# Four raw weight buffers in place of two during the attention stage of a fused attention and MoE kernel

## The chip, the cores and the metric

The kernel runs on one core of one Trainium2 chip. The metric is device time in microseconds (us) of one execution. The core has TensorE (PE in the profile, matrix products), VectorE (DVE) and ScalarE (ACT) for work on tiles, GpSimd (POOL), and SyncE (SP), whose queue issues nearly all the DMA transfers here.

## What is computed

Attention over 4 batches of 8 heads (576 positions, head size 64, causal, with a bias from cumulative sums), then two MoE-like layers on the 2304 x 512 result. The weights arrive as 64-bit floats and everything is computed to single-precision accuracy. Cut to what matters:

```python
def _attn_ref(q, k, v, s):
    scores = np.where(causal, -1e9, scale * q @ k.T + np.minimum(bias, 0.0))
    attn = exp(scores - max(scores)); attn /= sum(attn) + 1e-9
    return attn @ v
...
def _moe_ref(x, w1, w2, w3, w_out):
    return (x @ w1) * (x @ w2) @ w3 @ w_out
...
def _moe2_ref(x, w_in, w_out, g_ln):
    h = x @ w_in
    solu = h * softmax(h)
    return (layer_norm(solu) * g_ln) @ w_out
...
x = _attn_ref(...).transpose(0, 2, 1, 3).reshape(2304, 512)
return _moe2_ref(x=_moe_ref(x=x, ...), ...)
```

## The kernel before

**Stages.** The attention runs in 36 steps, one head a step: scores `sc` (L170, or L178 and L179 for later heads) on TensorE, softmax (L192 on VectorE, `L196` exp on ScalarE), normalisation (L225, L226, L233 on VectorE, L231 on ScalarE), transposes `tr` (L265 to L274) copied out to `PT` (L97 on VectorE, L95 on ScalarE), and the product `av` (L298). From step 10 on, pieces of the first MoE layer fill TensorE between these: `ab_unit` multiplies the attention's result by w1 (`a`) and w2 (`b`) at L326. ScalarE copies `a` out to `a_sb` (L338), and VectorE multiplies `b` by it into `g_sb` (L346), which frees the product's buffer in PSUM. After the attention come the last of these units with the product of w3 and w_out (L637), then the second layer: L721, L753, the normalisation, and L847.

**Weight blocks.** Weights come in blocks of 128 x 512 numbers of 64 bits, 512 KB each. `stage` (L398 to L409) takes a tile named `stage` from a pool and issues the load from SyncE's queue at L407. `to_f32` (L360 to L378) makes 32-bit floats of it in place, one scaling on ScalarE (L363) and three steps on VectorE (L369, L370, L374); `split_w` then writes a coarse part (`hi`, L95, ScalarE) and a rest (`lo`, L100, VectorE) as the two W tiles that the matmuls read. The last of these, the rest, frees the raw tile. L369 can only start when the block has landed. For the second layer's blocks `to_f32` writes its result to another tile (`cst`) at L374, which frees the raw tile.

**How many and when.** 16 blocks of w1 and w2 come first, then 8 of w_in, then 8 of the second w_out. The table `PUMP` (L551) says how many conversions are written into each step: one in steps 3, 5 and 6, two in steps 10 to 15, one in step 16, one each in steps 22 to 29, two each in 30 to 33. `pump` (L415) loads ahead as long as fewer blocks are under way than the pool has buffers, converts one, and loads again. After the attention, blocks come from another pool with four buffers (L616).

**What sets the order.** The engines' queues are in order. Which instruction stands where in its queue is decided when the kernel is built, by a scheduler of the framework that works with estimated durations, so an instruction whose input is estimated to be ready sooner is put sooner in its queue. `issue_after` adds an order: a conversion is put behind the first softmax tile of its step.

**GpSimd** has one task beside all this: `split_qk` (L160 to L163) writes the rest of the next head's Q and K (`lo`, L100 on POOL, QK from qk) after ScalarE's `hi` (L95).

Both numbers of buffers are at these lines:

```python
    stg = [at, 2]
...
        raw = stg[0].tile([128, CW, 2], U32, tag="stage", bufs=stg[1], name="stage")
...
        while jobs and len(loaded) < stg[1]:
...
    stg[:] = mp, 4
```

Of the kernel before, what the change touches and what calls it, by code (L numbers as in the profile page):

```python
# [26 lines left out]
def tile_attention_moe(  # L27
# [76 lines left out]
    at = attn_ctx.enter_context(tc.tile_pool(name="at", bufs=1, side="left"))  # L104
# [288 lines left out]
    jobs = []  # L393
    loaded = []

    stg = [at, 2]

    def stage(src):  # L398
        raw = stg[0].tile([128, CW, 2], U32, tag="stage", bufs=stg[1], name="stage")
# [619 lines left out]
```

## Time and profile before

| | us |
|---|---|
| median of 3 runs | 738.95 |
| the runs | 737.88 to 739.62 |
| the profiled execution | 737.73 |
| its span, first to last instruction | 736.0 |
| PE busy | 716.7 (97%) |
| DVE busy | 504.9 (69%) |
| ACT busy | 468.0 (64%) |
| POOL busy | 99.5 (14%) |

The granted TensorE clock is 0.997 of full speed over the span. A share of busy time is a mean over stages with different limits; what ends a wait in one stage is read from that stage's rows. In a row of a timeline, the brackets at the end give how long the engine stood idle before the instruction and what ended that idle time. "issue" there means that it waited for nothing that the profile shows.

### The profile page before, as it was taken

The numbers are of one execution on the slowest core, as the hardware profiler recorded it, in microseconds if no ns is written. First come the engines' busy times: TensorE is split into PE (matmuls) and PEld (weight loads), VectorE is DVE, ScalarE is ACT, GpSimd is POOL, SyncE is SP. The second block draws the span as 40 slices with busy tenths as digits, with TensorE's granted clock in tenths as the row PEclk, the third lists the DMA queues.
The fourth block names the chain that finished last, engine by engine and source line by source line (L and its number), as shares of the span: only waits on it lengthen the run. The fifth ranks groups of instructions, "written<-read, shape, count | busy, mean of one in ns | idle before, by whom it ended". The sixth has DMA issues, their size and how long they took to land.

```text
span 736.0 us, 13040 instructions
## 1 busy us (share of the span) xinstructions
PE 716.7 (97%) x4682; PEld 625.0 (85%) x4682; DVE 504.9 (69%) x1267; ACT 468.0 (64%) x985; POOL 99.5 (14%) x102
## 2 busy tenths in 40 slices
PE   9889998999999999999998999999999999999997
PEld 6567978888888899899997889988888988888886
DVE  7987978897678888632887876576747365563651
ACT  4987777898766777732544745577646465564652
POOL 5033313142221331000000000001000000000000
PEclk9999999999999999999999999999999999999999
DMA  4644554655476665614566943253234142304221
GB/s 109 186 126 99 174 161 142 194 144 130 127 221 186 182 188 149 208 61 147 170 215 202 355 149 101 58 110 75 79 82 101 44 123 75 89 12 75 44 57 44
DMA packets 79829, 95.52 MB, mean 130 GB/s; under 512 B 41418, under 2 KB 52682, under 8 KB 79764
## 3 DMA queue, kind: packets, MB, share of 16 engines
q1 hardware_dynamic: 79764, 94.69, 45.0%
q8 instruction: 37, 0.61, 0.3%
q14 instruction: 28, 0.23, 0.1%
HBM read 59.04 MB, written 20.14 MB: 108 GB/s over the span
## 4 chain that ended last, share of the span: by engine, by line
PE 73%; DVE 11%; DMA 8%; ACT 5%; issue 2%; POOL 1%; SPq 0%; ACTq 0%; DVEq 0%; POOLq 0%
PE x L721 14%; PE o L847 13%; PE b L326 10%; PE a L326 10%; PE hX L753 5%; DMA stage<-in_w_dram 5%; PE av L298 4%; PE hZ L753 3%; PE tr L265 3%; ACT P L196 2%; PE sc L170 2%; PE sc L178 2%; DVE P L192 2%; DVE stage L374 2%; PE hW L753 2%
## 5 line engine op out<-in xcount | busy, mean ns | idle before, releaser
L196 ACT ACTIVATE P<-P,STAT 128x576 f32<-128x576 f32 (+4 forms) x160 | 88.3, 554 | 31.5 <-DVE STAT L192 30.9
L100 POOL TENSOR_TENSOR QK<-qk,QK 64x1152 fp32r<-64x1152 f32 x24 | 67.1, 2798 | 167.2 <-ACT QK L95 158.9
L721 PE MATMUL x<-gl,MH 128*128 128x256 f32 x288 | 80.4, 280 | 0.0
L721 PE MATMUL x<-gh,ML 128*128 128x256 f32 x288 | 80.2, 279 | 0.0
L721 PE MATMUL x<-gh,MH 128*128 128x256 f32 x288 | 79.9, 280 | 0.0
L192 DVE CUSTOM_DVE_ANT_0 P<-sc,wmask 128x576 f32<-128x576 f32 (+4 forms) x160 | 70.6, 478 | 4.5 <-PE sc L170 3.2
L326 PE MATMUL a<-xT0h,W 128*128 128x288 f32 x256 | 58.1, 300 | 1.9 <-ACT a_sb L338 1.9
L326 PE MATMUL b<-xT0h,W 128*128 128x288 f32 x256 | 57.6, 299 | 1.5 <-DVE STAT L192 0.8
L847 PE MATMUL o<-OH,lh 128*128 128x512 f32 x144 | 57.1, 397 | 0.2 <-DVE ll L100 0.2
L326 PE MATMUL a<-xT1h,W 128*128 128x288 f32 x256 | 57.2, 298 | 0.0
L847 PE MATMUL o<-OH,ll 128*128 128x512 f32 x144 | 57.0, 396 | 0.0
L847 PE MATMUL o<-OL,lh 128*128 128x512 f32 x144 | 57.0, 396 | 0.0
L326 PE MATMUL b<-xT1h,W 128*128 128x288 f32 x256 | 56.5, 295 | 0.0
L721 PEld LDWEIGHTS x<-gl,MH 128*128 128x128 f32 x288 | 54.2, 188 | 1.3
L817 DVE COPY lt<-turned 128x2048 uint16<-128x2048 uint16 x16 | 21.9, 1368 | 48.4 <-DMA turned<-half 48.4
L721 PEld LDWEIGHTS x<-gh,MH 128*128 128x128 f32 x288 | 54.0, 188 | 1.1
L721 PEld LDWEIGHTS x<-gh,ML 128*128 128x128 f32 x288 | 54.1, 188 | 0.9
L346 DVE TENSOR_TENSOR g_sb<-b,a_sb 128x288 f32<-128x288 f32 x64 | 28.8, 449 | 32.8 <-PE b L326 16.7
L363 ACT ACTIVATE stage<-stage 128x512 f32<-128x512 f32 x56 | 36.9, 674 | 21.2 <-DMA stage<-in_w_dram 18.0
L298 PE MATMUL av<-PT,VT 128*64 128x64 f32 (+4 forms) x384 | 50.1, 395 | 0.0
L231 ACT ACTIVATE P<-P,STAT 128x576 f32<-128x576 f32 x64 | 42.7, 717 | 10.4 <-DVE STAT L226 10.4
L338 ACT ACTIVATE a_sb<-a 128x288 f32<-128x288 f32 x64 | 25.6, 401 | 33.3 <-PE a L326 33.1
(193 smaller groups left out, 1965.5 us busy)
## 6 DMA issues: line engine op xcount, KB each, us to landing
stage<-in_w_dram SPq DMA_DIRECT2D x32, 512.0 KB
g_scr<-g_sb SPq DMA_DIRECT2D x32, 288.0 KB
stage<-in_wo_dram SPq DMA_DIRECT2D x16, 512.0 KB
qk<-in_qk_dram SPq DMA_DIRECT2D x24, 288.0 KB
QK<-QK SPq DMA_DIRECT2D x24, 288.0 KB
gl<-g_scr SPq DMA_DIRECT2D x24, 256.0 KB
wf<-wf_scr SPq DMA_DIRECT2D x22, 256.0 KB
out_dram<-o SPq DMA_DIRECT2D x18, 256.0 KB
```

The lines of the kernel that those rows point to most:

```text
L100: eng.tensor_tensor(out=dst, in0=src, in1=hi_.bitcast(F32), op=ALU.subtract)
L192: mx = nc.vector.tensor_tensor_reduce(out=dst2, in0=ps_in, in1=msk, scale=-SCALE, scalar=BIG, op0=ALU.add, op1=ALU.min, accum_out=st[0:row ...
L196: ex = nc.scalar.activation(out=dst, in_=dst, func=AF.Exp, bias=st[0:rows, ti:ti + 1], scale=-1.0, accum_out=st[0:rows, 5 + ti:6 + ti],)
L231: nc.scalar.activation(out=dst, in_=dst, func=AF.Copy, scale=r)
L298: nc.tensor.matmul(st["ps"][64 * e:64 * e + 64, 448 + c0:448 + c1], vr[:, j, e], PT[(2 * p + e) % 4][:, o + c0:o + c1], **kw,)
L326: nc.tensor.matmul(ps, w_[:, c, fs], x_[:, c, sl], start=(c == 0 and w_ is WH and x_ is XH), stop=(c == KC - 1 and w_ is WL),)
L338: ab_last[0] = nc.scalar.activation(out=a_sb, in_=ps, func=AF.Copy).ins
L346: ab_last[1] = nc.vector.tensor_tensor(out=g[:, sl], in0=ps, in1=st["a"], op=ALU.mult).ins
L363: nc.scalar.activation(out=high.bitcast(F32), in_=high.bitcast(F32), func=AF.Copy, scale=2.0 ** -112)
L721: last = nc.tensor.matmul(ps[:, a], w_[:, k, m * 128:m * 128 + 128], g_[:, k % 2], start=(k == 0 and w_ is MH and g_ is GH), stop=(k == KF ...
L753: last_h[0] = nc.tensor.matmul(ps, x_[:, k], w_[:, k], start=first and k == 0 and x_ is XH and w_ is WH, stop=k == 1 and x_ is XL, skip_gr ...
L847: nc.tensor.matmul(ps, l_[:, k], w_[:, k], start=(k == 0 and l_ is LH and w_ is OH), stop=(k == KF - 1 and l_ is LL),)
```

## The change

One number: the pool of the attention stage gives the raw weight tiles four buffers in place of two. The loads ahead follow the same number (L413), so up to four blocks are under way.

```diff
-    stg = [at, 2]
+    stg = [at, 4]
```

No instruction of the work is added or removed. The first row of block loads in SyncE's queue holds four loads where it held two, ahead of the same rows of the next head, and later loads stand two blocks earlier. The scheduler's order of the conversions moves as well. Three places in VectorE's queue follow. Each W pair is named by its two tiles (W_123 the coarse part, W_124 the rest).

The first is the stretch before the g_sb at 88.97 us of the profile. Before:

```order
L192 ISA STAT_117 64x1
L100 TENSOR_TENSOR W_124<-stage,W_123 128x4x128
L192 ISA P,STAT_117<-sc,wmask 128x320
L192 ISA STAT_117 128x1
L192 ISA P,STAT_117<-sc,wmask 128x192
L192 ISA STAT_117 128x1
L100 TENSOR_TENSOR W_122<-stage,W_121 128x4x128
L346 TENSOR_TENSOR g_sb<-b,a_sb 128x288
```

And now:

```order
L192 ISA STAT_117 64x1
L370 SCALAR_TENSOR_TENSOR stage<-stage 128x512
L192 ISA P,STAT_117<-sc,wmask 128x320
L192 ISA STAT_117 128x1
L192 ISA P,STAT_117<-sc,wmask 128x192
L192 ISA STAT_117 128x1
L370 SCALAR_TENSOR_TENSOR stage<-stage 128x512
L100 TENSOR_TENSOR W_122<-stage,W_121 128x4x128
L374 SCALAR_TENSOR_TENSOR stage<-stage 128x512 x2
L346 TENSOR_TENSOR g_sb<-b,a_sb 128x288
```

Two L370 and two L374 of the next two blocks (numbers 8 and 9) now stand ahead of the g_sb; their two L369 stand ahead of it too, some rows earlier, together with the L100 of W_124. Before, all six stood behind it.

The second is some ten rows later, at 93 to 95 us, a piece of the difference with - for before and + for now:

```order
+L100 TENSOR_TENSOR W_124<-stage,W_123 128x4x128
+L97 COPY PT_111<-tr 64x64
+L100 TENSOR_TENSOR W_126<-stage,W_125 128x4x128
+L97 COPY PT_111<-tr 64x2x64
 L233 TENSOR_SCALAR P<-P,STAT_117 128x320
 L233 TENSOR_SCALAR P<-P,STAT_117 128x192
 L233 TENSOR_SCALAR P<-P,STAT_117 64x64
-L97 COPY PT_111<-tr 64x64
-L97 COPY PT_111<-tr 64x2x64
-L374 SCALAR_TENSOR_TENSOR stage<-stage 128x512
```

The two L100 that end blocks 8 and 9 stand here now, where before a step L374 of block 8 stood; the next L374 stands behind the next g_sb now and stood ahead of it.

The third is at 132 to 136 us, the stretch around two g_sb. Before:

```order
L369 TENSOR_SCALAR stage<-stage 128x512
L346 TENSOR_TENSOR g_sb<-b,a_sb 128x288
L369 TENSOR_SCALAR stage<-stage 128x512
L346 TENSOR_TENSOR g_sb<-b,a_sb 128x288
L97 COPY PT_111<-tr 128x512
```

And now:

```order
L97 COPY PT_111<-tr 128x512
L369 TENSOR_SCALAR stage<-stage 128x512
L100 TENSOR_TENSOR W_128<-stage,W_127 128x4x128
L346 TENSOR_TENSOR g_sb<-b,a_sb 128x288
L100 TENSOR_TENSOR W_126<-stage,W_125 128x4x128
L346 TENSOR_TENSOR g_sb<-b,a_sb 128x288
```

The copy of the transposes moved ahead, and an L100 of a block whose other steps are done stands ahead of each g_sb, where an L369 stood ahead of each.

## Rows read from the trace of the kernel before

**Rows 1.** the page, busy time of each engine, share of the span, instructions

```profile
PE 716.7 (97%) x4682; PEld 625.0 (85%) x4682; DVE 504.9 (69%) x1267; ACT 468.0 (64%) x985; POOL 99.5 (14%) x102
```

**Rows 2.** busy time in two stretches: us, then each engine, clock, DMA share

```profile
60.00:165.00 105.00, 99.71 (x759) 88.78 (x757) 89.45 (x260) 85.62 (x215) 28.36 (x10) 1.00 0.54 156
165.00:300.00 135.00, 135.00 (x1066) 120.60 (x1063) 104.25 (x310) 102.12 (x256) 33.44 (x13) 1.00 0.61 174
```

**Rows 3.** waits from 60 to 165 us: total us, times, longest us

```profile
DVE stage L369 <- DMA stage<-in_w_dram: 10.0, 8, 3.1
...
ACT stage L363 <- DMA stage<-in_w_dram: 4.1, 3, 2.8
```

**Rows 4.** TensorE in order: start us, us, operation [idle before <-releaser]

```profile
89.47 0.40 PE L326 MATMUL b<-xT0h,W 128*128 128x288 f32 x1 [0.65 <-DVE g_sb L346]
...
123.76 0.37 PE L178 MATMUL sc<-QK 128*128 128x288 f32 x1 [1.60 <-issue]
...
125.20 0.40 PE L326 MATMUL a<-xT0h,W 128*128 128x288 f32 x1 [0.67 <-ACT a_sb L338]
...
134.83 0.41 PE L274 MATMUL tr<-ident,P 64*64 64x64 f32 x4 [0.42 <-DVE g_sb L346]
...
310.96 0.40 PE L326 MATMUL a<-xT0h,W 128*128 128x288 f32 x1 [1.20 <-ACT a_sb L338]
```

**Rows 5.** steps on a block: duration in ns, min/median/max

```profile
L369 DVE TENSOR_SCALAR stage<-stage x56: 382/422/2034, 22.3 to 431.3; 128x512 uint32<-128x512 uint32 x56
L363 ACT ACTIVATE stage<-stage x56: 647/668/766, 24.6 to 429.5; 128x512 f32<-128x512 f32 x56
L370 DVE SCALAR_TENSOR_TENSOR stage<-stage x56: 642/684/821, 25.3 to 432.8; 128x512 uint32<-128x512 uint32 x56
L374 DVE SCALAR_TENSOR_TENSOR stage<-stage x40: 673/685/1848, 26.0 to 434.6; 128x512 uint32<-128x512 uint32 x40
...
L100 DVE TENSOR_TENSOR W<-stage,W x16: 643/677/2461, 29.0 to 155.0; 128x512 fp32r<-128x512 f32 x16
```

**Rows 6.** VectorE in order of time, 77 to 89 us

```profile
77.99 0.43 DVE L369 TENSOR_SCALAR stage<-stage 128x512 uint32<-128x512 uint32 x1 [0.83 <-DMA stage<-in_w_dram]
...
84.02 1.96 DVE L100 TENSOR_TENSOR W<-stage,W 128x512 fp32r<-128x512 f32 x1
...
86.59 2.46 DVE L100 TENSOR_TENSOR W<-stage,W 128x512 fp32r<-128x512 f32 x1
88.97 0.44 DVE L346 TENSOR_TENSOR g_sb<-b,a_sb 128x288 f32<-128x288 f32 x1
```

**Rows 7.** GpSimd in order of time

```profile
82.74 5.76 POOL L100 TENSOR_TENSOR QK<-qk,QK 64x1152 fp32r<-64x1152 f32 x2 [13.42 <-ACT QK L95]
...
131.46 2.67 POOL L100 TENSOR_TENSOR QK<-qk,QK 64x1152 fp32r<-64x1152 f32 x1 [4.06 <-ACT QK L95]
```

**Rows 8.** chain of waits from 60 to 165 us: start us, us, what

```profile
89.08 3.98 DMA stage<-in_w_dram
```

**Rows 9.** VectorE in order of time, 93 to 133 us

```profile
93.08 0.43 DVE L369 TENSOR_SCALAR stage<-stage 128x512 uint32<-128x512 uint32 x1 [0.53 <-DMA stage<-in_w_dram]
...
105.47 0.47 DVE L369 TENSOR_SCALAR stage<-stage 128x512 uint32<-128x512 uint32 x1 [1.18 <-DMA stage<-in_w_dram]
109.05 0.43 DVE L369 TENSOR_SCALAR stage<-stage 128x512 uint32<-128x512 uint32 x1 [3.11 <-DMA stage<-in_w_dram]
...
122.91 0.74 DVE L192 CUSTOM_DVE_ANT_0 P<-sc,wmask 128x576 f32<-128x576 f32 x1
...
132.38 2.03 DVE L369 TENSOR_SCALAR stage<-stage 128x512 uint32<-128x512 uint32 x1 [1.64 <-DMA stage<-in_w_dram]
```

**Rows 10.** ScalarE at 310 us

```profile
309.93 0.68 ACT L363 ACTIVATE stage<-stage 128x512 f32<-128x512 f32 x1 [1.33 <-DMA stage<-in_wo_dram]
```

**Rows 11.** SyncE's DMA queue, then TensorE, on the early load

```profile
18.97 0.47 SPq L129 DMA_DIRECT2D qk<-in_qk_dram  x1
...
29.91 1.13 PE L170 MATMUL sc<-qk 128*128 128x288 f32 x4
```

## The prediction

> **What bounds the kernel now.** I read the busy shares first: TensorE is busy 716.7 us of a 736.0 us span [rows 1]. Nothing can gain more than the 19.3 us in which it stands still, and of these only the part that raw weight blocks cause. So I next read the stretches. From 60 to 165 us, where thirteen of the sixteen w1 and w2 blocks are converted, PE is busy 99.71 of 105.00 us: 5.29 us idle. From 165 to 300 us, with further blocks converted beside it, it is busy 135.00 of 135.00 [rows 2]. An added buffer can gain nothing in that second stretch; a delay made before it is carried through it whole, since PE has no pause in which to catch up.
>
> The waits of the first stretch come next: VectorE stands 10.0 us before L369, ScalarE 4.1 us before L363, each for a weight block to land [rows 3]. That is the wait which the change removes, 14.1 us on two engines, but PE is idle only 5.29 us there. The list of PE's pauses says what it waited for: 0.65 us at 89.47 for the eviction g_sb, 1.60 at 123.76 (named "issue"; VectorE's L192 beside it, 122.91 plus 0.74, ends 0.11 us earlier [rows 9]), 0.67 at 125.20 for a_sb, 0.42 at 134.83 for g_sb; later, 1.20 at 310.96 for a_sb [rows 4]. PE never waits for a weight block itself. It waits for an eviction that stands behind a conversion in VectorE's or ScalarE's queue, and these queues are in order. The longest block wait, 3.11 us at 109.05 [rows 9], has no pause of PE beside it. So the time is decided by what stands ahead of an eviction, and the change moves that too.
>
> **The change part by part.** The same loads and conversions are issued; only their order differs. A block is four steps on VectorE and two on ScalarE; their median durations are in [rows 5]. I cost places, not totals. My unit is PE's idle time, before and after, and each difference goes into the end one for one, because of the full stretch behind.
>
> *First loads.* Two more blocks are issued at 18 us, ahead of the rows qk of the next head. Those are issued at 18.97 and the first product that reads them starts at 29.91 [rows 11]: 10.94 us. One block took 3.98 us from issue to use in the chain of waits [rows 8]; alone on the queue two more cost at most 7.96, and that head's own load, if it takes no more than such a block, makes 11.94 of it: between nothing and 1.0 us late. I take nothing: the transfers run on 16 engines at once, and 3.98 includes a latency that is not paid twice.
>
> *Around 89 us (term a).* In the new order blocks 8 and 9 are converted ahead of the g_sb that PE's pause at 89.47 waits for. Ahead of it now stand two L369 (0.42 each), two L370 (0.68) and two L374 (0.69), 3.58 us [rows 5]; the block wait of 0.83 at 77.99 goes [rows 6], net 2.75. This must be weighed against GpSimd. Two VectorE steps L100 there took 1.96 and 2.46 us [rows 6] where such a step's median is 0.68 [rows 5], and they end as GpSimd's two L100 do (82.74 plus 5.76 is 88.50) [rows 7]: VectorE was held for 3.06 us. Behind 88.50 the new order still has the second L370, one L100, two L374 and the g_sb: 0.68 + 0.68 + 1.37 + 0.37 = 3.10, so g_sb ends at 91.6 and not at 89.34 (88.97 plus 0.37, where the next step starts): +2.26. If ScalarE's two L363 that now stand before the next QK step put GpSimd off by their 2 x 0.67 = 1.34 [rows 5], it is +3.6; if the second L370 slips in ahead of GpSimd's second step, +1.6. I take the middle, **+2.6**.
>
> The Trainium skill ("SBUF — State Buffer", section Who interferes with whom) says that a VectorE instruction with two SBUF inputs and a GpSimd instruction that reads SBUF block each other entirely, the later one waiting for the whole of the earlier. The two long L100 agree with it; no row before shows an L370 so held, though it has two SBUF inputs as well. By that rule a is +2.26 or more; if an L370 is not held, the second one runs inside the hold and a is its 0.68 less, +1.6.
>
> *From 90 to 107 us (term b).* Between that g_sb and the next pauses the order gains two L100 (2 x 0.68) and loses two L374 (2 x 0.69), which is even. What is left is a wait: block 11 can be loaded only when block 7's L100 frees its buffer, which still stands just before the g_sb, at about 90.5. A load takes 3.98 [rows 8], so it lands near 94.5, and VectorE reaches its L369 between 93.3 and 93.9: 0.6 to 1.2 us of waiting where there were 0.53 at 93.08 [rows 9]. Middle **+0.4**, ends 0 and +1.5 (a hold by GpSimd that falls on one of the L100: 1.96 less 0.68 is 1.3).
>
> *From 105 to 126 us (term c).* By now loads are two blocks further ahead, and the waits of 1.18 and 3.11 us at 105.47 and 109.05 go [rows 9]. VectorE reaches its L192 of 122.91 earlier, and the 1.60 and 0.67 us of PE go: **-2.27**. This also pays for a part of the lag from a: VectorE, which was late by a, catches up in 4.29 us of former waiting, PE does not. Ends: -2.27, and -1.60 where only the first goes.
>
> *Around 134 us (term d).* VectorE waited 1.64 us there and its L369 then took 2.03 (GpSimd ran from 131.46 for 2.67) [rows 7, 9]; both go, but an L100 is put ahead of the two g_sb, and could be held in its place. PE's 0.42 may go, or grow by up to a whole hold, 2.67. I take **0**, ends -0.4 and +2.7.
>
> *Around 311 us (term e).* ScalarE waits 1.33 us for a block of the second w_out in front of the a_sb that PE waits 1.20 us for [rows 10, 4]. The last of these loads also come two blocks earlier in the order, and the wait goes: **-1.2**, ends -1.2 and 0 (another wait takes its place).
>
> The blocks after the attention had four buffers already; their waits stay. Sum: 2.6 + 0.4 - 2.27 + 0 - 1.2 = -0.47. The profiled execution took 737.73 us, 1.7 of it outside the span; it would take 737.3. The median of the runs lies 1.22 above the profiled one, 738.95, so the forecast for it is **738.5 us**. With all lows the sum is 1.6 + 0 - 2.27 - 0.4 - 1.2 = -2.3, with all highs but d (3.6 + 1.5 - 1.6 + 0 + 0) +3.5: this case's own range is 736.7 to 742.5.
>
> **The rivals.**
> *Every load-made pause goes, no new one comes.* VectorE has 105.00 - 89.45 = 15.55 us free in the stretch [rows 2], more than all moved steps take; if the early conversions only use free time, all 5.29 us and the 1.20 us go: -6.5, 732.5 us; with half of it, 735.7. For it: the waits of 10.0 and 4.1 us. Against it: at 77 to 89 us, where blocks 8 and 9 are put, VectorE has no free time but the 0.83.
>
> *Earlier conversions delay evictions: slower.* A conversion that is ready sooner is put in the queue sooner, among softmax tiles and ahead of g_sb. Place: 81 to 89 us, with GpSimd's 5.76 us; price: a at 3.6, b at 1.5, and d at +2.7, less c and e at their small end, -1.6 and 0: +6.2 at worst, 745.2; with d at 0, +3.5, 742.5. It decides once a and b together exceed 3.5 us, what c and e together give back. For it: 135 us without a pause in which a lag could shrink. Against it: VectorE gets 4.29 us back at 105 to 109.
>
> *The waits were hidden anyway.* PE's pauses then come from the order of evictions alone and reappear elsewhere: 0, 738.95.
>
> That the change does nothing it says (the loads not issued earlier) I leave at nothing: the order shows four loads in the first row where there were two.
>
> **How the numbers follow.** About 0.2%, 1.5 us, is what a measurement of this kernel can tell from no change; same is 737.5 to 740.4. Chances: my forecast 0.45, of which 0.11 ends below 737.5 and 0.10 above 740.4; every pause goes 0.25, all faster; slower 0.23, all slower; waits hidden anyway 0.07, same. Faster 0.36, same 0.31, slower 0.33. The range leaves out the lower part of the first rival (below 734.6) and the upper part of the second (above 742.8), a tenth each: 734.6 to 742.8. Both signs hold most of the chance, so the likeliest case's own range, 736.7 to 742.5, is to be kept beside it.
>
> **What would show it.** The waits before L369 for w1 and w2 blocks from 60 to 165 us fall from 10.0 to at most 2 us: if not, the loads are late for another reason. The g_sb behind blocks 8 and 9 ends 1.6 to 3.6 us later against its PE step, and PE pauses there for more than 2 us: if it pauses under 1 us, term a is wrong, and the first rival holds. An L370 or L374 of 1.8 us or more lies beside GpSimd's L100. The pauses at 123.76, 125.20 and 310.96 are gone: if one stays, c or e is wrong. PE still has none between 165 and 300 us; if it has, the delay is not carried one for one, and the whole sum is wrong.

## The result and the profile after

With four buffers the kernel is slower. The median of 6 runs is 743.73 us (740.96 to 745.29), against 738.82 us (6 runs) for the kernel before; the ratio is 1.0063, 95% interval 1.0041 to 1.0084. The profiled execution took 742.21 us, its span is 740.4 us against 736.0.

Of the page of the changed kernel, the busy time of each engine (answers [rows 1]), and below it two stretches with the same columns as [rows 2]:

```profile
PE 720.1 (97%) x4682; PEld 629.0 (85%) x4682; DVE 508.2 (69%) x1267; ACT 467.6 (63%) x985; POOL 98.8 (13%) x102
...
60.00:165.00 105.00, 96.89 (x708) 86.14 (x705) 88.42 (x246) 81.09 (x199) 25.36 (x9) 0.95 0.52 154
165.00:300.00 135.00, 135.00 (x1064) 122.00 (x1063) 105.59 (x309) 102.19 (x258) 35.71 (x13) 1.00 0.57 162
```

The same 4682 matmuls are busy for 720.1 us in place of 716.7. So in this pair of executions, of the 4.4 us by which the span grew, 3.4 are matmuls that ran slower and only 1.0 is time in which PE stood still (20.3 us in place of 19.3). The column behind the five engines goes with it: the granted clock is 0.95 in the first stretch, where it was 1.00. How far this holds beyond this pair is asked in the first experiment.

The waits for weight blocks are gone as forecast: between 60 and 165 us no wait for a load stands before an L369 or an L363 any more [rows 3]. The waits list of that stretch (total us, times, longest us) now has, among others, these:

```profile
PE b L326 <- DVE g_sb L346: 5.5, 2, 2.8
ACT W L95 <- DVE stage L374: 5.0, 5, 2.4
```

TensorE's pauses, in order of time, as in [rows 4]:

```profile
80.91 0.47 PE L178 MATMUL sc<-QK 128*128 128x448 f32 x1 [0.93 <-DVE g_sb L346]
...
93.38 0.40 PE L326 MATMUL b<-xT0h,W 128*128 128x288 f32 x1 [2.65 <-DVE g_sb L346]
...
107.45 0.40 PE L326 MATMUL b<-xT0h,W 128*128 128x288 f32 x1 [1.71 <-DVE STAT L192]
...
132.35 0.58 PE L326 MATMUL b<-xT0h,W 128*128 128x288 f32 x1 [2.81 <-DVE g_sb L346]
```

The small pauses of before have become one of 0.93 us and three long ones. The first is a matter of place alone: its g_sb stood ahead of an L370 and an L374 before (at 79.10 us, with no pause of PE) and stands behind them now (at 80.41), and GpSimd runs nothing beside them. For the three long ones, VectorE's rows ahead of them show what is late, and GpSimd's rows what ran beside it (start, us, operation):

```profile
85.39 2.70 DVE L370 SCALAR_TENSOR_TENSOR stage<-stage 128x512 uint32<-128x512 uint32 x1
...
88.70 2.45 DVE L370 SCALAR_TENSOR_TENSOR stage<-stage 128x512 uint32<-128x512 uint32 x1
...
92.88 0.44 DVE L346 TENSOR_TENSOR g_sb<-b,a_sb 128x288 f32<-128x288 f32 x1
...
103.48 2.70 DVE L374 SCALAR_TENSOR_TENSOR stage<-stage 128x512 uint32<-128x512 uint32 x1
...
126.39 3.17 DVE L374 SCALAR_TENSOR_TENSOR stage<-stage 128x512 uint32<-128x512 uint32 x1
```

```profile
84.84 5.75 POOL L100 TENSOR_TENSOR QK<-qk,QK 64x1152 fp32r<-64x1152 f32 x2 [15.07 <-ACT QK L95]
102.36 3.27 POOL L100 TENSOR_TENSOR QK<-qk,QK 64x1152 fp32r<-64x1152 f32 x1 [11.76 <-ACT QK L95]
...
126.06 2.95 POOL L100 TENSOR_TENSOR QK<-qk,QK 64x1152 fp32r<-64x1152 f32 x1 [2.92 <-ACT QK L95]
```

Each long step of VectorE, 0.68 us by its median [rows 5], lies beside one GpSimd instruction and ends 0.55 us behind its end. Ahead of the first pause two L370 are held, ahead of the second an L374, ahead of the third another.

The clock ahead of the pauses and behind them, by stretches with the columns of [rows 2]; the column behind POOL's is the granted clock, and 0.50 is its lower level, 1.2 GHz. First the changed kernel, then the kernel before:

```profile
90.70:93.30 2.60, 0.03 (x1) 0.00 (x0) 2.60 (x6) 1.90 (x7) 0.00 (x0) 1.00 0.20 60
...
94.10:97.40 3.30, 3.30 (x16) 3.30 (x15) 2.85 (x13) 2.70 (x6) 0.00 (x0) 0.50 0.63 199
97.50:98.10 0.60, 0.60 (x7) 0.60 (x6) 0.60 (x3) 0.41 (x1) 0.00 (x0) 1.00 0.00 0
...
132.40:138.40 6.00, 6.00 (x25) 5.79 (x26) 6.00 (x13) 4.38 (x8) 1.45 (x1) 0.50 0.48 135
```

```profile
89.40:92.70 3.30, 3.23 (x24) 3.23 (x25) 3.14 (x14) 3.30 (x11) 0.00 (x0) 1.00 0.88 231
...
396.50:400.00 3.50, 3.50 (x10) 2.71 (x9) 3.04 (x6) 2.41 (x4) 0.00 (x0) 0.51 0.37 114
```

In 3.3 us PE does 16 matmuls where it did 24. Behind the pause at 93.38 the same run of work, from the first matmul of that `b` to the first matmul of the next `b`, goes from 93.38 to 98.19 (4.81 us); before it went from 89.47 to 92.76 (3.29 us). The lower clock costs 1.52 us there. The last row shows that the trace of before had the pattern already, behind its longest pause, 2.05 us at 395.72. The changed kernel has that stretch too, near 401 us, and one more at 53 to 56 us, which cost little, since PE waited 1.05 us there before and does no more.

How far the last transposes (L267) of some heads lie behind the kernel before:

| start before, us | start after, us | later by, us |
|---|---|---|
| 62.70 | 63.15 | 0.45 |
| 88.41 | 89.21 | 0.79 |
| 97.03 | 102.46 | 5.44 |
| 121.61 | 126.65 | 5.04 |
| 134.16 | 142.23 | 8.07 |
| 165.38 | 172.27 | 6.89 |
| 208.41 | 214.99 | 6.57 |
| 309.35 | 315.92 | 6.57 |
| 320.32 | 325.51 | 5.19 |
| 494.47 (L847) | 498.95 | 4.48 |

The loss is made twice, at 88 to 97 and at 122 to 134 us. The 0.79 us understates the lag there: four score products (L178 and L179, 89.38 to 90.31) stand behind that L267 now and stood ahead of it before, and the last matmul of `a` ahead of both lies 1.29 us behind (87.85 against 86.56). Of the 8.07 us 1.5 come back by 208 us; nothing of the 6.57 that are left is given back through the rest of the full stretch; 1.38 come back at 311 us, where the pause of 1.20 [rows 4] is gone, and 0.7 more later.

### The profile page after: what moved, and what is told of

It is laid out like the page before. It is cut to its first block, busy times and chain, and to the rows that moved or that the text cites. A ratio compares the mean times of both kernels' runs of the same rounds, so it can differ in the third digit from the quotient of the medians.

```text
span 740.4 us, 13031 instructions
## 1 busy us (share of the span) xinstructions
PE 720.1 (97%) x4682; PEld 629.0 (85%) x4682; DVE 508.2 (69%) x1267; ACT 467.6 (63%) x985; POOL 98.8 (13%) x102
## 4 chain that ended last, share of the span: by engine, by line
PE 89%; DVE 6%; ACT 2%; issue 2%; POOL 1%; DMA 0%; SPq 0%; ACTq 0%; POOLq 0%
PE x L721 14%; PE o L847 13%; PE b L326 13%; PE a L326 13%; PE av L298 6%; PE m L637 6%; PE hX L753 5%; PE tr L265 4%; PE hZ L753 3%; PE sc L178 2%; PE sc L170 2%; PE sc L179 2%; PE hW L753 2%; PE hY L753 2%; DVE stage L374 1%
## 5 line engine op out<-in xcount | busy, mean ns | idle before, releaser
L100 POOL TENSOR_TENSOR QK<-qk,QK 64x1152 fp32r<-64x1152 f32 x24 | 66.4, 2769 | 174.1 <-ACT QK L95 174.0
L192 DVE CUSTOM_DVE_ANT_0 P<-sc,wmask 128x576 f32<-128x576 f32 (+4 forms) x160 | 70.6, 479 | 6.4 <-PE sc L170 3.6
L326 PE MATMUL a<-xT0h,W 128*128 128x288 f32 x256 | 59.7, 306 | 0.0
L847 PE MATMUL o<-OH,lh 128*128 128x512 f32 x144 | 57.0, 396 | 0.2 <-DVE ll L100 0.2
L847 PE MATMUL o<-OH,ll 128*128 128x512 f32 x144 | 57.0, 396 | 0.0
L847 PE MATMUL o<-OL,lh 128*128 128x512 f32 x144 | 57.0, 396 | 0.0
L326 PEld LDWEIGHTS b<-xT0h,W 128*128 128x128 f32 x256 | 43.6, 191 | 8.3 <-ACT PT L95 3.0
```

The costliest lines, as they stand in the source:

```text
L100: eng.tensor_tensor(out=dst, in0=src, in1=hi_.bitcast(F32), op=ALU.subtract)
L192: mx = nc.vector.tensor_tensor_reduce(out=dst2, in0=ps_in, in1=msk, scale=-SCALE, scalar=BIG, op0=ALU.add, op1=ALU.min, accum_out=st[0:row ...
L326: nc.tensor.matmul(ps, w_[:, c, fs], x_[:, c, sl], start=(c == 0 and w_ is WH and x_ is XH), stop=(c == KC - 1 and w_ is WL),)
L847: nc.tensor.matmul(ps, l_[:, k], w_[:, k], start=(k == 0 and l_ is LH and w_ is OH), stop=(k == KF - 1 and l_ is LL),)
```

## Experiments

The theory after the result: the loads are harmless, and the order that they allow puts two-input VectorE steps beside GpSimd's L100 and ahead of evictions; these holds make pauses of PE, and the clock falls behind some long pauses. A step is called held when it takes longer than its median beside a GpSimd instruction. Ratios below are to the kernel before as measured beside each run, with 95% intervals; medians of different runs come from different chips, so the ratios are compared. All kernels whose text says nothing else compute everything.

**Are the loads to blame?** Four buffers, two blocks loaded ahead. VectorE's, TensorE's and GpSimd's orders stay those of the changed kernel; only SyncE's rows differ.

```diff
-        while jobs and len(loaded) < stg[1]:
+        while jobs and len(loaded) < (2 if stg[0] is at else stg[1]):
```

> Four buffers as in the changed kernel, but only two blocks are loaded ahead where the program asks for loads: SyncE's first row of block loads holds two, and the order on VectorE, TensorE and GpSimd is that of the changed kernel. Theory (the order of the conversions makes the kernel slower, not the loads): 743 to 745 us, and the pauses of TensorE near 93, 107 and 132 us stay. Rival (the earlier loads disturb something): 738 to 740 us, with those pauses gone or halved.

Measured: 742.66 us, 1.0047 (1.0028 to 1.0066), and the pauses stay: 2.38 at 93.50, 2.15 at 108.03 and 2.81 at 132.91. The number is a little under what the theory said, the loss is the same within the intervals. The four loads at 18 us are not the cause.

This run also weighs the clock, since the orders of the engines are those of the changed kernel. Its profiled execution has a span of 740.9 us, and its busy times are:

```profile
PE 717.7 (97%) x4682; PEld 626.2 (85%) x4682; DVE 508.5 (69%) x1267; ACT 467.9 (63%) x985; POOL 98.2 (13%) x102
```

The three pauses are there, but behind the one at 132.91 the clock stays up (1.00 from 133 to 140 us). The span is 4.9 us longer than before, and of these only 1.0 is busy time and 3.9 are idle. So nearly the whole loss comes without that stretch of lower clock, and the 3.4 of 4.4 us above belong to one pair of executions, with granted clocks of 0.997 and 0.988 over the span. The mean over all runs differs less: 0.990 for the six of the changed kernel, 0.992 for the ten of this run, 0.993 to 0.994 for the kernel before beside the experiments.

**Is it the hold or the place?** GpSimd's L100 on Q and K becomes a fill that reads nothing, in the changed kernel and in the kernel before.

```diff
-        lo(t[64:128, 1::2], raw, t[64:128, 0::2], G)
+        nc.gpsimd.memset(t[64:128, 1::2].bitcast(F32), 0.0)
```

> The changed kernel with GpSimd's L100, which reads SBUF and computes the rest of Q and K, replaced by a fill of the same tile with zeros, which reads nothing: the rest is left out, so scores are rougher. VectorE's order is that of the changed kernel but for a few rows. Theory (the moved L370 and L374 cost much because GpSimd holds them, and long pauses of TensorE bring its clock down): no L370 or L374 over 1 us, the pauses near 93, 107 and 132 us shrink by 1.5 to 2 us each, the stretches at half clock go, 735 to 739 us. Rival (their place alone, in front of evictions): pauses shrink by less than 0.7 us each and 742 to 744 us.

> The kernel before with the same replacement of GpSimd's L100 by a fill with zeros (the rest of Q and K is left out). VectorE's order is that of the kernel before but for a few rows. Theory: the held L100 (1.96, 2.46 and 1.79 us) go back to 0.7, but PE pauses there are short, so only 0.5 to 2 us are gained: 736.5 to 738.5 us; and the changed kernel without GpSimd's reads is as fast as this one or up to 3 us faster. Rival (place alone): 737 to 739, and the changed kernel without the reads stays 4 us or more above it.

Measured: 735.37 us, 0.9954 (0.9934 to 0.9974), for the changed order; 737.24 us, 0.9967 (0.9936 to 0.9998), for the order of before. In the first of these kernels the L370 and the g_sb that follows are:

```profile
85.05 0.68 DVE L370 SCALAR_TENSOR_TENSOR stage<-stage 128x512 uint32<-128x512 uint32 x1
...
86.34 0.68 DVE L370 SCALAR_TENSOR_TENSOR stage<-stage 128x512 uint32<-128x512 uint32 x1
...
88.76 0.44 DVE L346 TENSOR_TENSOR g_sb<-b,a_sb 128x288 f32<-128x288 f32 x1
```

The g_sb comes 4.12 us earlier than at 92.88, and PE has no pause there. The changed kernel gained 1.1% by the fill, the kernel before 0.3%. So in sum the place alone costs nothing: with the fill the changed order is level with the order of before or slightly ahead. At one spot the place does cost: the pause of 0.93 us at 80.91 stays (0.94 at 80.57). And one part of the forecast failed. Instead of a smaller pause near 107 us with the clock up, the profiled execution, the slowest of its ten, has this one, with the clock at half from 100.5 to about 107 us:

```profile
100.52 0.63 PE L274 MATMUL tr<-ident,P 64*64 64x64 f32 x4 [2.03 <-DVE STAT L192]
```

Ahead of it VectorE waited 2.37 us for a weight block, at 93.90; that this wait made the pause is not shown.

These two kernels leave work out, and the fill is also shorter (1.05 to 1.24 us where the L100 took 2.7 to 3.3), so the next pair does all of the work.

**Short holds with all the work.** GpSimd's instruction is issued as eight pieces. In the changed kernel VectorE's order stays as it was up to 160 us; in the kernel before it differs in some rows from 90 us on. (The new line is broken in two here.)

```diff
-        lo(t[64:128, 1::2], raw, t[64:128, 0::2], G)
+        [lo(t[64:128, 1 + 2 * i, s_], raw[:, i, s_], t[64:128, 2 * i, s_], G)
+         for i in range(2) for s_ in (slice(c, c + S // 4) for c in range(0, S, S // 4))]
```

> The changed kernel, complete, with GpSimd's L100 on Q and K issued as eight pieces of 64x144 in place of one of 64x1152; VectorE's order up to 160 us is that of the changed kernel. Theory (a VectorE step is held until the GpSimd instruction beside it ends): each hold falls from up to 2.7 us to the rest of one piece, no L370 or L374 over 1.2 us, the pauses near 93, 107 and 132 us lose 1.5 us each, 736 to 739 us. Rival (what the kernel without GpSimd's reads gained came from the computation it left out, or from Q and K being ready sooner): 742 us or more, since GpSimd then takes as long as before or longer.

> The kernel before with the same eight pieces on GpSimd. Theory: its holds fall too, but few pauses of PE hang on them: 737 to 738.5 us, 0.3 to 1.5 us faster than before. Together with the changed kernel in eight pieces: the change is then worth between 1 us slower and 2 us faster. Rival (the change costs time by its place alone): the two in eight pieces stay 4 us or more apart.

Measured: 734.48 us, 0.9936 (0.9914 to 0.9957), with four buffers, faster than both kernels; 740.02 us, 1.0012 (0.9987 to 1.0037), with two. The first is better than forecast; the second gained nothing where 0.3 to 1.5 us were forecast; and the change is worth 5.5 us between the two, by their medians, where 2 at most were. For VectorE and GpSimd in the first kernel (start, us, operation):

```profile
85.30 0.68 DVE L370 SCALAR_TENSOR_TENSOR stage<-stage 128x512 uint32<-128x512 uint32 x1
...
86.59 0.76 DVE L370 SCALAR_TENSOR_TENSOR stage<-stage 128x512 uint32<-128x512 uint32 x1
87.27 0.98 DVE L100 TENSOR_TENSOR W<-stage,W 128x512 fp32r<-128x512 f32 x1
88.17 1.87 DVE L374 SCALAR_TENSOR_TENSOR stage<-stage 128x512 uint32<-128x512 uint32 x2
89.97 0.44 DVE L346 TENSOR_TENSOR g_sb<-b,a_sb 128x288 f32<-128x288 f32 x1
```

```profile
84.75 10.30 POOL L100 TENSOR_TENSOR QK<-qk,QK 64x144 fp32r<-64x144 f32 x16 [13.15 <-ACT QK L95]
```

GpSimd now needs 10.30 us for what took 5.75, and the kernel is faster: VectorE's steps run between the pieces or are held for one of them only, and GpSimd has time. That Q and K were ready sooner can't be the reason here, as it could with the fill: GpSimd ends later (95.05 us) than in the changed kernel (90.59). With two buffers VectorE's waits before L369 grow instead, in a listing by line from 60 to 170 us (count, busy us and mean ns, idle before and its releaser), the kernel in pieces below the kernel before:

```profile
L369 DVE TENSOR_SCALAR stage<-stage 128x512 uint32<-128x512 uint32 x13 | 7.3, 568 | 10.1 <-DMA stage<-in_w_dram 10.0
```

```profile
L369 DVE TENSOR_SCALAR stage<-stage 128x512 uint32<-128x512 uint32 x13 | 6.2, 486 | 15.1 <-DMA stage<-in_w_dram 15.1
```

That two buffers in pieces gain nothing because VectorE then waits for loads is argued from these two rows and not shown: no run takes these waits away by itself, VectorE's order differs from 90 us on, and in this execution the clock is also at half from 53.5 to 60.5 and from 128.5 to 132.5 us, where it is up in the kernel before. What is shown is that the two changes don't add: buffers alone lose 0.6%, pieces alone change nothing that can be told, both together gain 0.6%.

**How short must a piece be?** Two pieces, VectorE's order as in the changed kernel.

> The changed kernel with two pieces on GpSimd in place of one; VectorE's order is that of the changed kernel. Theory (a hold is the rest of one GpSimd instruction): holds up to 1.4 us, less than half the gain of the eight pieces kept at most, between 735 and 740 us, and no pause over 2 us. If GpSimd's next piece follows before VectorE gets in, the hold is two pieces and the time that of the changed kernel, 742 to 744 us.

Measured: 742.53 us, 1.0067 (1.0052 to 1.0082; 4 runs), all of the changed kernel's time; the second expectation holds in its number, though not by its mechanism. GpSimd and the held steps:

```profile
86.72 6.91 POOL L100 TENSOR_TENSOR QK<-qk,QK 64x576 fp32r<-64x576 f32 x4 [14.93 <-ACT QK L95]
```

```profile
90.47 1.90 DVE L100 TENSOR_TENSOR W<-stage,W 128x512 fp32r<-128x512 f32 x1
92.30 2.49 DVE L374 SCALAR_TENSOR_TENSOR stage<-stage 128x512 uint32<-128x512 uint32 x2
```

No step is held for two pieces: the two L370 take 1.44 and 1.24 us. But the L100 and the first L374 (1.89 us) are held now too, which ran free behind GpSimd's end in the changed kernel. The work alternates, and with pieces of 1.7 us (6.91 by four) the holds ahead of g_sb, less 0.68 us a step, come to the same sum, 3.75 us against 3.79; PE's pause is 2.35 us.

**Which holds?** Four buffers and eight pieces, but at named heads the whole instruction; VectorE's order is that of the kernel in eight pieces up to 160 us. The heads in the condition change from run to run; the last run has `h in (11, 12, 13, 15)`.

```diff
         for i in range(2) for s_ in (slice(c, c + S // 4) for c in range(0, S, S // 4))]
+        if h not in (15,) else lo(t[64:128, 1::2], raw, t[64:128, 0::2], G)
```

> Four buffers and eight pieces on GpSimd for all heads but one, head 15, whose L100 is one whole instruction again: it is the one that lay beside the held L374 of 3.17 us at 126.39 in the changed kernel. VectorE's order is that of the kernel in eight pieces. Theory (one hold at one place makes the pause of 2.81 us at 132, and the pause brings the half clock behind it): one L374 of about 3 us, a pause of 2 to 3 us near 130, the clock at half for 3 to 7 us behind it, and 2.5 to 5 us more than the kernel in eight pieces, 737 to 739.5 us. Rival (the holds act only together): under 1.5 us more, 734.5 to 736 us.

> The same with heads 11 and 12 whole, whose two L100 hold the two L370 of blocks 8 and 9 at 85 to 91 us in the changed kernel. Theory: the L370 take 2.4 to 2.7 us again, the pause near 93 is 2 to 2.7 us with the half clock behind it, 2 to 4.5 us more than the kernel in eight pieces, 736.5 to 739 us; less if the free time of VectorE at 110 to 120 us takes a part back. Rival (the holds act only together): under 1.5 us more.

> Eight pieces on GpSimd but for head 13, whole. Theory (each held place costs its pause, 1 to 3 us): an L374 of about 2.7 us near 101, a pause of PE near 104 of 1 to 2 us, 1 to 2.5 us more than the 734.5 us of the kernel in eight pieces. Rival (only holds together): under 1 us more.

> Eight pieces but for heads 11, 12, 13 and 15, whole. If the places add up: 1.2 + 2.9 + 1 to 2.5 us above 734.5, 739.6 to 741.1 us. If they build on each other, by a later start of every step behind and by the clock: 742 to 744 us, all of the changed kernel's time. If the rest lies at other heads: 737 to 739 us.

> Whole at all heads but 11, 12, 13 and 15, which are in eight pieces. If these four places carry the loss: 734 to 736 us. If other heads carry it: 738 us or more.

| whole at heads | median, us | ratio (95%) | above 0.9936 |
|---|---|---|---|
| 15 | 735.72 | 0.9970 (0.9952 to 0.9988) | 0.34% |
| 11, 12 | 737.42 | 0.9986 (0.9967 to 1.0005) | 0.50% |
| 13 | 735.56 | 0.9960 (0.9942 to 0.9977) | 0.24% |
| 11, 12, 13, 15 | 740.55 | 1.0029 (1.0007 to 1.0050) | 0.93% |
| all but these four | 736.66 | 0.9969 (0.9953 to 0.9984) | 0.33% |
| all (the changed kernel) | 743.73 | 1.0063 (1.0041 to 1.0084) | 1.27% |

The places add as far as this can tell: 0.34 + 0.50 + 0.24 is 1.08 against 0.93, and 0.93 + 0.33 is 1.26 against 1.27; but each ratio has an interval of about 0.2% to either side, so single places are rough. By these ratios the four places carry about three quarters. The four together, 740.55 us, lie in the range for places that add up. Head 15 alone missed its forecast: 735.72 us lies in the range of the rival, 734.5 to 736. Heads 15 and 13 cost 1.2 and 1.1 us by medians, 2.5 and 1.8 by ratios, the low end of what was expected or below it, and the kernel with these four in pieces at 736.66 lay between the two expectations. Head 15 alone made its pause, but with the clock up behind it (the last row, with the columns of [rows 2]):

```profile
128.47 0.37 PE L326 MATMUL b<-xT0h,W 128*128 128x288 f32 x1 [2.31 <-DVE g_sb L346]
```

```profile
128.50:132.00 3.50, 3.50 (x27) 3.41 (x28) 3.50 (x9) 2.44 (x6) 0.00 (x0) 1.00 0.29 91
```

So the half clock doesn't follow every pause of that length; with heads 11 and 12 whole it does follow a pause of 2.29 us (0.50 from 93 to 96 us). Which pauses it follows stays open.

**Three buffers**, whole and in eight pieces.

```diff
-    stg = [at, 4]
+    stg = [at, 3]
```

> Three buffers. The first L370, L370 and L374 in the crowded stretch stand as in the changed kernel, but only one block, not two, is put ahead of the g_sb that PE's b waits for near 90 us, and later places lie between the two kernels. Theory (the number of two-input steps put beside GpSimd and ahead of g_sb decides): between the two, 739.5 to 742.5 us. Rival (any look-ahead beyond two costs the same): 743 to 745 us.

> Three buffers with eight pieces on GpSimd. Theory: three buffers already were near the kernel before because their holds make no long pause; with short holds they come to 734 to 736.5 us, as four buffers with eight pieces do. Rival (the fourth buffer is needed for the gain): 737 us or more.

Measured: 737.79 us, 0.9986 (0.9969 to 1.0003), and 732.91 us, 0.9945 (0.9927 to 0.9963). The first is a miss: three buffers are not between the two kernels but level with the kernel before. Ahead of the g_sb of 92 us two steps are held there too, an L370 for 2.44 us at 85.39 and an L100 for 2.46 at 88.44, but no more than in the kernel before (two L100, 1.96 and 2.46 us [rows 6]), and PE pauses 0.26 us for that g_sb. The longest pause between 60 and 165 us is 1.63 us, and the clock stays at full speed behind it. Within the intervals three buffers in pieces are as fast as four; the fourth is not needed.

**Other places for the conversions.** In both kernels four buffers, the table of conversions changed.

```diff
-    PUMP = {3: 1, 5: 1, 6: 1, 10: 2, 11: 2, 12: 2, 13: 2, 14: 2, 15: 2, 16: 1}
+    PUMP = {3: 1, 4: 1, 5: 1, 6: 1, 7: 2, 8: 2, 9: 2, 10: 1, 11: 1, 12: 1, 13: 1, 14: 1, 15: 1}
```

> Four buffers, and the table that says how many conversions are written into each step is spread: one in steps 4 to 6 each and step 3, two in steps 7 to 9, one in steps 10 to 15, where it was none in steps 4 and 7 to 9 and two in steps 10 to 15. Theory (too many conversions at once in the crowded stretch from 76 to 140 us): the pauses near 93, 107 and 132 us go, no half clock after 60 us, 733 to 737 us. Rival (earlier loads and conversions as such make it slower): 743 us or more.

```diff
-    PUMP = {3: 1, 5: 1, 6: 1, 10: 2, 11: 2, 12: 2, 13: 2, 14: 2, 15: 2, 16: 1}
+    PUMP = {3: 1, 5: 1, 6: 1, 10: 2, 11: 2, 13: 2, 14: 2, 15: 2, 16: 2, 17: 1}
```

> Four buffers, and the conversions of steps 12 to 16 written one step later (steps 13 to 17). Ahead of the g_sb near 89 us then stand one L374 and two L100 of earlier blocks, about as in the kernel before, while loads stay four ahead. Theory (place and hold decide): the pause at 93 us falls to under 1.2 us, with no half clock behind it; 739 to 742 us, since L370 and L374 still meet GpSimd near 125 us. Rival (four buffers and early loads cost by themselves): 743 to 745 us.

Measured: 741.92 us, 1.0027 (1.0007 to 1.0048), and 742.17 us, 1.0049 (1.0018 to 1.0080). The first is a miss. The pauses near 93 and 107 us are gone and that at 132 falls to 1.19, as forecast, but the loss has moved to where the conversions went: 2.75 us at 58.14 before `tr`, with VectorE's copies behind conversions, and half clock from there to 67 us, where none was forecast after 60. The second, 0.2 us above its range, removes the first long pause (0.45 is left at 93.64) and gets two others: 2.35 at 120.96, released by GpSimd's QK, and 2.82 at 124.94, released by the W of an L95, so by a block that is now converted too late. Why QK came late in the first of them stays open. This run doesn't tell the theory from its rival.

## Why the prediction was wrong

**The bound and the full stretch: right.** The waits for blocks went to nothing, PE still has no pause from 165 to 300 us, and from 208 to 309 us the lag is carried unchanged. Term e was -1.2 and measured -1.38.

**Term a: the mechanism right, one consequence missing.** The g_sb ended 3.91 us later (93.25 against 89.34), 2.6 to 3.1 after the lag of 0.79 to 1.29 that was there already: inside 1.6 to 3.6. The L370 were held, 2.70 and 2.45 us, and the runs in pieces and with the fill take the holds away. The Trainium skill ("SBUF — State Buffer", section Who interferes with whom) has it so for a step with two SBUF inputs beside a GpSimd instruction that reads SBUF, and the trace agrees. PE's pause grew by 2.0 us. What the sum lacked is the clock, 1.5 us behind this pause in the profiled execution, and the new pause of 0.93 us at 80.91.

**Term b** was +0.4; from 97 to 122 us, the stretch of b and the first part of c, the lag changed by -0.4. The wait for block 11 on which it rested did not come.

**Term c is the step that failed.** It took PE's pauses of 1.60 and 0.67 us for gone, -2.27. They went, but a longer one came. The same L374 stands beside the same GpSimd instruction in both kernels. Before, it started 0.22 us ahead of it, took 0.68 us (the first of the two in this row), and GpSimd's instruction took 3.59:

```profile
123.59 1.28 DVE L374 SCALAR_TENSOR_TENSOR stage<-stage 128x512 uint32<-128x512 uint32 x2
```

```profile
123.81 3.59 POOL L100 TENSOR_TENSOR QK<-qk,QK 64x1152 fp32r<-64x1152 f32 x1 [6.03 <-ACT QK L95]
```

Now it starts at 126.39, 0.33 us behind GpSimd's start at 126.06, and is held for 3.17 us ahead of the next g_sb. PE paused for 2.81 us and then, in this execution, ran at half clock until 138.4. Where c had -2.27, the lag grew by 3.0 from 122 to 134 us. I had weighed the moved steps against GpSimd's rows at 83 and 131 us only; the order showed moved L370 and L374 at every head between.

**Term d** was 0; the pause of 0.42 us went, its low end, and the lag fell by 0.7 to 144 us and by 0.8 more to 208.

**The clock had no term at all.** The kernel before shows the lower level once, behind its pause of 2.05 us at 395.72, so it could have been priced. In the profiled pair 3.4 of the 4.4 us are busy time, but the run with two blocks ahead loses 4.9 us with 1.0 of busy time: idle time makes most of that loss, and what the clock costs on average was not measured.

By the lag in the table, the sum of -0.47 became 4.48. Term c alone missed by 5.3 us (3.0 in place of -2.27) and term a by about 2 (4.65 from 88 to 97 us in place of 2.6); the rest went the other way. The second rival, that earlier conversions delay evictions, had the mechanism, and its 742.5 to 745.2 us hold the median; but it put the loss at 81 to 89 us and counted c as a gain of 1.6, so its meeting the number is partly luck. My own range ended 0.9 us under the median. Every sign that I had named came true; none of them looked for a new pause between 97 and 131 us.

## What to carry to other kernels

A buffer that takes a wait away also lets a scheduler move the work that waited, and that work must be checked for every place where it now lands: what stands behind it in the queue, and what runs beside it on GpSimd. A step that starts a few tenths of a microsecond ahead of a GpSimd instruction in one order can start behind it in the next. Where PE is nearly always busy, give the clock behind a long pause a term of its own, from nothing to what such a stretch cost in the trace at hand. When two changes touch the same queue, try them together: buffers lost 0.6%, short GpSimd instructions changed nothing, and both gained 0.6%.

## What the runs showed of the hardware

A GpSimd instruction cut into eight takes much longer in all, 10.30 us for two heads where 5.75 sufficed (most pieces take 0.49 to 0.51 us, and sixteen such make 8.0; those beside a conversion step of VectorE take up to 1.14), and still the kernel gains; cut into two it gains nothing.

It is what GpSimd does, and not only that it runs, which holds a two-input step. With the fill, which reads nothing, an L370 beside it keeps its time:

```profile
122.70 0.64 DVE L370 SCALAR_TENSOR_TENSOR stage<-stage 128x512 uint32<-128x512 uint32 x1
```

```profile
122.55 1.06 POOL L162 MEMSET QK<- 64x1152 f32 x1 [3.07 <-PE sc L179]
```

Steps of VectorE with one tensor read from SBUF are held as well: L369 took 2.03 us beside a GpSimd L100 in the kernel before, where its median is 0.42 [rows 9, 5]. In the kernel with head 15 whole, normalisation (L233, three instructions) met GpSimd where L374 had met it in the changed kernel, and took as long:

```profile
122.58 0.69 DVE L374 SCALAR_TENSOR_TENSOR stage<-stage 128x512 uint32<-128x512 uint32 x1
123.19 3.17 DVE L233 TENSOR_SCALAR P<-P,STAT 128x320 f32<-128x320 f32 x3
```

The softmax tiles (L192) and g_sb, which read PSUM, keep their time beside the same GpSimd instructions: the g_sb at 89.97 in the kernel in pieces takes 0.44 us, and an L192 of 128 x 320 in the changed kernel, at 88.02 between the two held L370, takes 0.48, as in the kernel before (85.90).
